# Pacing the dense pieces of an attention training step by TensorE time, fusing the q, k and v transposes, loading operand slabs by quarter, and moving VectorE work to ScalarE and GpSimd

## The chip, the cores and the metric

The kernel runs on one core of a Trainium2 chip. The metric is device microseconds of one execution. A ratio of two kernels is the mean time of the fast runs of one over the mean of the fast runs of the other, both from the same rounds on the same chip, so it is not quite the ratio of the medians that are quoted beside it. "About the same" means within 2%.

## The reference, cut to what matters

The program is forward and backward of four layers over 2048 tokens of width 640 with 32 heads of 20: linear attention (A), window attention (B), A, B. It returns the output and the gradients of the input and of the four weight matrices.

```python
def _A_ref(x, wqkv, wo):            # linear attention
    ...
    pq, pk = phi(q), phi(k)
    kv = jnp.einsum("bhsd,bhse->bhde", pk, v)
    ...
    return (num / den) ... @ wo

def _B_ref(x, wqkv, wo):            # causal window of 256
    scores = jnp.einsum("bhqd,bhkd->bhqk", q, k) * (Dh ** -0.5)
    mask = (idx[:, None] - idx[None, :] >= 0) & (idx[:, None] - idx[None, :] < W)
    p = _softmax(jnp.where(mask[None, None], scores, -1e9), axis=-1)
    return jnp.einsum("bhqk,bhkd->bhqd", p, v) ... @ wo

x = x + _A_ref(_layernorm(x), A_wqkv, A_wo)
x = x + _B_ref(_layernorm(x), B_wqkv, B_wo)     # and the same pair once more
```

## The kernel before

A tile is 128 tokens, so there are 16 tiles. Two kinds of stage matter here. A *forward pair* runs the output side of layer A, the whole layer B and the first side of the next layer A. A *window backward* runs the backward of layer B, in eight chunks of two tiles, with the output-side backward of B ahead of it and the rest of the backward behind it.

Both are written in the same way. A main sequence of short attention *steps* (8 per forward tile, 32 per chunk) needs ScalarE, VectorE and GpSimd between its matmuls. Between two steps the program emits *pieces* of dense work (projections, transposes, layer norms) from generators, so that TensorE has something to do while a step waits. Each `yield` ends a piece. The kernel before gives out pieces **by count**:

```python
def drive(main, fills):             # fills: (generator, pieces per step, delay)
    live = [[f[0], f[1], 0.0, f[2] if len(f) > 2 else 0] for f in fills]
    for _ in main:                  # one step of attention
        for f in live:
            f[3] -= 1
            if f[0] is None or f[3] >= 0:
                continue
            f[2] += f[1]
            while f[2] >= 1.0:
                f[2] -= 1.0
                if next(f[0], StopIteration) is StopIteration:
                    f[0] = None
                    break
    ...                             # what is left is emitted at the end

# forward pair, tile t: the front of a later tile and the back of the one before
    fills.append((take(ahead, 17), 17 / G))              # G = 8 steps
    fills.append((prev, 14 / (G - 2), 2))
    drive(self.b_core(st, lb, t, o), fills)

# window backward, chunk c
    fills.append((before(c + 1), 18 / 32))
    fills.append((behind(c - 2), 36 / 25, 7))            # two chunks late, from step 7
    drive(core(c), fills)
```

The pieces that make q, k and v of a forward tile, with a DMA transpose for q and k as soon as they are there, and one for v at the end:

```python
hn = self.ln(st, l, t, x)                                # VectorE, one piece
yield
hnT = self.flip(st.ps, st.sb, hn, "hnT", P, DT, P, nc.vector)
yield
for j, nm in enumerate("qkv"):
    for c in range(2):
        ps = self.dense(st, hnT, W, j * D + c * CW)      # 5 matmuls of 320 columns
        ...                                              # copy to R["s"] on VectorE
        yield
    if j == 1:
        self.dma(R["T"][:, 0:2, :, :]..., R["s"][:, 0:2, :, :]..., transpose=True)
self.dma(sv["s"][t], R["s"]...)
self.dma(R["T"][:, 2, :, :], R["s"][:, 2, :, :]..., transpose=True)
self.dma(sv["T"][t], R["T"]...)
```

In the window backward, half of the transposes of `ds` are done on TensorE and copied out of PSUM by VectorE; the others go by DMA. The trailing pieces `behind(c)` begin with a transposing DMA that reads what an earlier DMA stored (`dqT<-dqkv`), and their matmuls read `dqT`.

```python
nc.vector.tensor_copy(v(dT), v(ps))                      # dsT, VectorE
...
nc.vector.tensor_tensor(out=pr[:, hs, :], in0=self.heads(ps[:, 0:CW]),   # product for delta
                        in1=self.heads(o[:, c * CW:(c + 1) * CW]), op=ALU.mult)
...
with self.tc.high_priority():                            # score matmuls, exponential and ds
    ...                                                  # are placed ahead of the pieces
```

The order of instructions on an engine is fixed when the program is built, by a scheduler that takes the order of emission and these priorities.

The softmax here doesn't subtract the row's maximum and nothing guards it: scores larger than these inputs give would overflow.

## Time and profile before

| | us |
|---|---|
| time, median of 3 runs | 2978.84 (2966.33 to 2979.95) |
| profiled run | 2969.4 |
| forward: both pairs, from about 124 us to the first exponential of the first window backward | 843 |
| windows: both window backwards, each from its first exponential to its close | 1296 |
| the rest: first layer, two linear backwards, weight gradients | 830 |

These stage lengths are read from the trace by the start times of the instructions named; the forward stages begin at the first write of `mz`, at about 124 us.

First, three lines of the page of the kernel before: TensorE's busy time with its share of the span, and the granted TensorE clock and the DMA share by fortieths of the span, in tenths.

```profile
PE 2296.9 (77%) x28216; PEld 1520.9 (51%) x28216; DVE 1649.3 (56%) x3436; ACT 1104.7 (37%) x1693; POOL 775.9 (26%) x1584
...
PEclk9988888778886557777776985677877769989799
...
DMA  6264554456566567777655985676776457379852
```

TensorE is the busiest engine, and its clock is lower where the window backwards are. The next view gives busy time by stretch for the kernel before: first pair, second pair, first window backward. The columns are length, then busy us and number of instructions of PE, PEld, DVE, ACT and POOL, then the mean granted clock, the DMA share and GB/s.

```profile
124.00:585.00 461.00, 370.79 (x4800) 247.36 (x4798) 275.73 (x735) 214.05 (x227) 170.26 (x282) 0.85 0.50 143
585.00:944.00 359.00, 277.47 (x4131) 183.33 (x4130) 177.78 (x467) 176.26 (x129) 159.82 (x263) 0.81 0.59 162
944.00:1623.00 679.00, 499.32 (x7248) 333.66 (x7248) 450.66 (x744) 274.72 (x480) 214.99 (x500) 0.70 0.67 148
```

In the forward pairs TensorE is far ahead of the others; in the windows VectorE comes close to it (450.66 against 499.32 us). What TensorE waits for is told by the waits of the kernel before: total us, number, longest. First in the steady part of the second pair (660 to 900 us), then in four steady chunks of the first window backward (1172 to 1474 us).

```profile
PE ops L162 <- DVE ob L411: 8.2, 11, 0.8
PE flip L208 <- DVE o L318: 8.2, 12, 0.7
PE flip L208 <- DVE hn L229: 7.4, 12, 0.6
PE sT L162 <- DMA T<-s: 6.8, 12, 1.0
```

```profile
PE dp L162 <- DVE ds L655: 19.5, 35, 1.6
PE acc L162 <- DMA dsT<-ds: 13.2, 12, 2.4
PE dense L162 <- DMA dqT<-dqkv: 6.5, 4, 1.9
...
PE flip L661 <- DVE ds L655: 4.4, 8, 0.6
```

The forward waits are short and spread. In the windows the wait for `ds` on VectorE is the largest (by two readers, the product `dp` and the TensorE transposes `flip`: 23.9 us together), and that for the transposed `dsT` second.

### The profile page before, as it was taken

The page shows a single profiled execution, that of the slowest core. Times are in us where ns is not written, and L with a number is a line of the kernel's source. Part 1 is how long each engine was busy: PE and PEld are TensorE (multiplying, and loading weights), DVE is VectorE, ACT ScalarE, POOL GpSimd, SP SyncE. Part 2 cuts the span into 40 slices and gives each one's busy share as a digit, 9 for nine tenths or more (in the row PEclk, how much of TensorE's full clock was granted, in tenths as well). Part 3 has the DMA queues.
Part 4 walks back from the last instruction along what each step waited for, and adds up shares of the span by engine and source line. Part 5 has one row for each costly group of instructions (what it writes and reads, how often), then busy time and mean ns, then how long its engine had stood idle before and what let it go on. Part 6 is the DMA issues. An engine that isn't in the chain of part 4 may idle for free.

```text
span 2969.4 us, 68304 instructions
## 1 busy us (share of the span) xinstructions
PE 2296.9 (77%) x28216; PEld 1520.9 (51%) x28216; DVE 1649.3 (56%) x3436; ACT 1104.7 (37%) x1693; POOL 775.9 (26%) x1584
## 2 busy tenths in 40 slices
PE   5778888668885677877776856778777759968599
PEld 4455555445553455555554644555555536447454
DVE  6656666545552467777764654777777630037100
ACT  2245555325553344444441423444444300024000
POOL 2033443325553243333330003433433200000000
PEclk9988888778886557777776985677877769989799
DMA  6264554456566567777655985676776457379852
GB/s 231 95 175 140 145 158 146 133 160 164 160 167 159 163 136 147 163 150 163 136 128 152 272 218 159 141 155 166 165 162 129 102 167 228 117 207 262 270 161 73
DMA packets 737911, 484.46 MB, mean 163 GB/s; under 512 B 484160, under 2 KB 710464, under 8 KB 737600
## 3 DMA queue, kind: packets, MB, share of 16 engines
q1 hardware_dynamic: 737600, 480.10, 62.6%
q8 instruction: 222, 3.64, 0.5%
q14 instruction: 89, 0.73, 0.1%
HBM read 216.53 MB, written 146.54 MB: 122 GB/s over the span
## 4 chain that ended last, share of the span: by engine, by line
PE 29%; DMA 14%; DVE 8%; issue 8%; POOL 4%; ACT 2%; SPq 2%; POOLq 0%; ACTq 0%; DVEq 0%
PE wg L162 12%; PE dense L162 9%; DMA dsT<-ds 4%; DVE ds L655 4%; DMA dqT<-dqa 3%; DMA dqT<-dqkv 3%; PE dp L162 2%; POOL e L618 2%; PE acc L162 2%; SPq L134 2%; DMA dqkv<-dq 2%; POOL e L622 2%; PE flip L661 1%; PE flip L208 1%; ACT e L615 1%
## 5 line engine op out<-in xcount | busy, mean ns | idle before, releaser
L655 DVE TENSOR_TENSOR ds<-dp,e 128x768 bf16<-128x768 f32 (+2 forms) x512 | 462.3, 903 | 212.9 <-PE s L162 112.5
L615 ACT ACTIVATE e<-s 128x768 bf16<-128x768 f32 (+2 forms) x512 | 395.0, 771 | 496.0 <-PE s L162 362.3
L376 ACT ACTIVATE eT<-sT 128x1536 bf16<-128x1536 f32 (+2 forms) x256 | 351.0, 1371 | 343.5 <-PE sT L162 328.9
L618 POOL TENSOR_SCALAR_AFFINE_SELECT e<-e 128x256 bf16<-128x256 bf16 x512 | 214.7, 420 | 702.4 <-ACT e L615 681.6
L378 POOL TENSOR_SCALAR_AFFINE_SELECT eT<-eT 128x512 bf16<-128x512 bf16 x256 | 164.3, 642 | 417.2 <-ACT eT L376 417.0
L162 PE MATMUL acc<-qs,ds 128*128 128x20 bf16 x2880 | 259.6, 177 | 15.3 <-DVE dq L717 12.7
L162 PE MATMUL dp<-vT,dT 32*128 32x384 bf16 (+2 forms) x1024 | 208.6, 400 | 80.0 <-DVE ds L655 62.7
L162 PEld LDWEIGHTS <-dqT 128*128 128x128 bf16 x1920 | 183.4, 105 | 162.4 <-DMA dqT<-dqkv 42.2
L162 PE MATMUL acc<-ks,dsT 128*128 128x20 bf16 x2880 | 207.1, 177 | 71.2 <-DMA dsT<-ds 70.2
L162 PEld LDWEIGHTS <-hnT 128*128 128x128 bf16 x1920 | 194.3, 107 | 129.9 <-DVE hnT L213 27.1
L162 PE MATMUL wg<-rq,lh 128*128 128x480 bf16 x1280 | 259.5, 366 | 0.0
L162 PE MATMUL acc<-ds,e 128*128 128x20 bf16 x2880 | 255.0, 175 | 0.0
L939 DVE CAST wr<-wg 128x480 bf16<-128x480 f32 (+1 forms) x36 | 21.7, 602 | 369.8 <-PE wg L162 369.8
L162 PEld LDWEIGHTS <-ds 128*128 128x128 bf16 x2880 | 213.0, 101 | 20.3 <-issue 15.9
L162 PE MATMUL dense<-WTB,dqT 128*128 128x320 bf16 x960 | 185.0, 343 | 40.2 <-DMA dqT<-dqkv 39.6
L162 PEld LDWEIGHTS <-e 128*128 128x128 bf16 x2880 | 205.0, 101 | 18.4 <-issue 10.5
L162 PE MATMUL s<-kT,qT 32*128 32x384 bf16 (+2 forms) x1024 | 208.3, 404 | 1.5 <-ACT e L615 1.1
L661 PE MATMUL flip<-ident,ds 128*128 128x128 bf16 x1440 | 177.9, 265 | 38.6 <-DVE ds L655 35.4
L162 PEld LDWEIGHTS <-dsT 128*128 128x128 bf16 x2880 | 154.6, 102 | 101.4 <-DMA dsT<-ds 81.1
L162 PEld LDWEIGHTS <-lh 128*128 128x128 bf16 x1280 | 125.2, 98 | 133.7
L162 PE MATMUL dense<-WTA,dqT 128*128 128x320 bf16 x960 | 166.9, 311 | 33.3 <-DMA dqT<-dqa 33.3
L622 POOL TENSOR_SCALAR_AFFINE_SELECT e<-e 128x256 bf16<-128x256 bf16 x448 | 192.0, 429 | 0.0
(133 smaller groups left out, 4099.9 us busy)
## 6 DMA issues: line engine op xcount, KB each, us to landing
rq<-dqkv SPq DMA_DIRECT2D x16, 1920.0 KB, 9.5
s<-s SPq DMA_DIRECT2D x32, 768.0 KB, 4.3
T<-T SPq DMA_DIRECT2D x32, 768.0 KB, 3.6
dqkv<-dq SPq DMA_DIRECT2D x32, 480.0 KB, 3.8
dqkv<-dqa SPq DMA_DIRECT2D x32, 480.0 KB, 3.7
kT<-T SPq DMA_DIRECT2D x28, 512.0 KB, 3.7
vT<-T SPq DMA_DIRECT2D x28, 512.0 KB, 4.3
ks<-s SPq DMA_DIRECT2D x28, 512.0 KB, 4.4
```

The costliest lines, as they stand in the source:

```text
L134: return self.nc.sync.dma_start(out=out, in_=in_, transpose=transpose)
L162: return self.nc.tensor.matmul(out, lhsT=lhsT, rhs=rhs, start=start, stop=stop, skip_group_check=True, **kw)
L208: self.nc.tensor.transpose(t[0:w, j, :], src[:, c0:c0 + w], self.ident)
L376: nc.scalar.activation(e[:, :, 0:nb * P], s[:, :, 0:nb * P], ACT.Exp)
L378: nc.gpsimd.affine_select(out=dg, in_=dg, compare_op=ALU.is_ge, fill=0.0, base=0, pattern=[[0, 4], [1, P]], channel_multiplier=-1)
L615: ex = nc.scalar.activation(e[:, :, 0:cw], s[:, :, 0:cw], ACT.Exp)
L618: nc.gpsimd.affine_select(out=dg, in_=dg, compare_op=ALU.is_ge, fill=0.0, base=0, pattern=[[0, 2], [-1, P]], channel_multiplier=1)
L622: nc.gpsimd.affine_select(out=fr, in_=fr, compare_op=ALU.is_ge, fill=0.0, base=-1, pattern=[[0, 2], [1, P]], channel_multiplier=-1)
L655: st.frees.append(nc.vector.tensor_tensor(out=ds[:, :, 0:cw], in0=st.dp[:, :, 0:cw], in1=e[:, :, 0:cw], op=ALU.mult))
L661: nc.tensor.transpose(ps[:, 3 * j + i, :], ds[:, j, i * P:(i + 1) * P], self.ident)
L939: nc.vector.tensor_copy(r[:, 0:w], a[:, 0:w])
```

## The change

Its intent: give out pieces by the TensorE time they take, so that every step gets about the same; load the operands of the windows in fewer, longer DMAs; take work off VectorE in the windows. The core of the diff, with cuts:

```diff
-def drive(main, fills): ...
+class Pace:
+    def __init__(self, gen, rate): ...
+    def step(self):
+        self.acc = min(self.acc + self.rate, 2 * self.rate)
+        while self.acc > 0:
+            w = next(self.gen, StopIteration)
+            ...
+            if w is None:           # not yet: ends the step
+                return
+            self.acc -= w           # w: TensorE us of the piece
 ...
         hn = self.ln(st, l, t, x)
-        yield
+        yield 0.05
         hnT = self.flip(st.ps, st.sb, hn, "hnT", P, DT, P, nc.vector)
-        yield
+        yield 0.3
 ...                                 # dense pieces: yield 0.7; delta and its product: yield 0.02
-            if j == 1:
-                self.dma(R["T"][:, 0:2, :, :]..., transpose=True)
-        self.dma(R["T"][:, 2, :, :]..., transpose=True)
+        self.dma(R["T"]..., flat, transpose=True)         # q, k and v in one, at the end
 ...
+            fa = Pace(chain(*[front(t) for t in range(1, TT)]), 7.6 / G)
+            fb = Pace(behind(), 7.3 / G)
 ...
-                for nm, k, w in (("kT", "T", 1), ("vT", "T", 2), ("ks", "s", 1)): ...
-                for nm, k in (("qT", "T"), ("qs", "s")): ...
+                for nm in ("T", "s"):                     # q, k, v of 4 tiles, a quarter of the heads
+                    S[nm] = sl.tile([P, 4, 2, 3, P], BF, name="slab" + nm)
 ...
-            nc.vector.tensor_copy(v(dT), v(ps))
+            if (g + bi) % 2:
+                nc.scalar.copy(v(dT), v(ps))
+            else:
+                nc.vector.tensor_copy(v(dT), v(ps))
 ...
-            nc.vector.tensor_tensor(out=pr[:, hs, :], ...)   # per half, from PSUM
+        nc.gpsimd.tensor_tensor(out=pr, in0=dn[:, :, 0:DH], in1=self.heads(o), op=ALU.mult)
 ...
-                    fills.append((before(c + 1), 18 / 32))
-                    fills.append((behind(c - 2), 36 / 25, 7))
+            fb = Pace(all_behind(), 14.5 / 32)            # behind(c) from the moment c is stored
+                    paces.append(Pace(before(c + 1), 5.4 / 32))
```

The tiles of `dqT` and two other loads of the trailing pieces also get a second buffer. The fillers of the linear backwards are paced as well. I call the two moves off VectorE "the relief" below.

## The prediction

> What bounds the kernel now. Cutting the trace into stretches: first layer 0-124 us, two forward pairs 124-950 (826 us), two window-attention backwards (950-1624 and 1740-2427, 1361 us), two linear backwards about 236 us, weight gradients the rest. The change touches the forward pairs and the window backwards.
>
> Forward pair: TensorE is busy 371 of 462 us at a granted clock of 0.85; ScalarE (214) and VectorE (276) are below it. Window backward, steady part: 84 us per pair of tiles (32 steps), VectorE busy 63-67, TensorE 67 at clock 0.78, ScalarE 40. Its TensorE waits in 1118-1540: 28 us for ds on VectorE, 7 us for flip after ds, 20 us for the transposed dsT, 9 us for dqT. So TensorE is first, VectorE a close second. The clock records hold only 1.0 and 0.5; stretches with little matmul work in them are followed by 0.5. The Trainium skill's "TensorE: Matmul & The Clock Gate" (Part 1) says the same.
>
> What the change does.
> 1. Pacing. Read from the built instruction order: before, each forward tile has seven score groups with about 1.3 us (warm) of TensorE work between them, then one lump of 6.6 us. After, the lump is still there: 5.4-8.9 us in most tiles of the first pair, 2.2 in one; the tail after the last score group grows from 21 to 27 us. Work is unchanged. In the window backward the largest gap between score groups grows from 3.0 to 4.8 us. Worth: 0 to +10 us.
> 2. One transpose for q, k and v. Scores now wait for it after the last v piece; before they waited for q,k after the k pieces. TensorE has 3.0-4.0 us of work in between against 3.9 before, and the transpose is half as large again (T landed in a median 4.7 us). The wait "sT for T", 25 us over both pairs now, should roughly double: +15 to +30 us.
> 3. Slabs: per pair of tiles 6.3 MB instead of 4.2, in 1536 B rows rather than 1024 B. The 1024 B packets took 53 ns each and 14% of the DMA engines; I estimate 21%, DMA share 0.68 to 0.75. Waits for dsT: 0 to +10 us per window.
> 4. VectorE relief: per 84 us, eight dsT copies (0.55 us) to ScalarE and four products (0.48 us) to GpSimd: 6.3 us less, 10% of its work; its lumps between ds products shrink (4.3 to 3.6 us). ScalarE gets about 6 us more, with room. I expect a third to a half of the 35 us ds waits per window to go: -15 us each. Double-buffered dqT takes most of its 9 us: -8 us each.
> 5. The drain (about 73 us per window) gets the GpSimd product (1.35 us for 0.48) into a serial chain: +3 us each.
>
> Sum: forward +15 to +35, windows -50 to -10: near nothing.
>
> Predicted 2965 us, range 2885 to 3045. Faster by over 2%: 0.27; within 2%: 0.56; slower by over 2%: 0.17.
>
> What would show it: window stretches at 80-83 us per pair of tiles with VectorE near 58-60 busy; "dp for ds" waits clearly below 28 us; forward pairs unchanged or longer, with longer waits of sT on T; DMA share up 0.05-0.08 in the window.
>
> What would make it wrong: fewer VectorE stalls lifting the window clock well above 0.78 (faster); the fused transpose costing less because the score groups run further ahead (faster); low-work runs of steps dropping the clock, or slab bursts delaying dsT (slower).

## The result, and the profile after

The changed kernel took 3095.28 us in the median of three runs (3090.24 to 3097.12); the ratio to before is 1.040, with a 95% interval of 1.0354 to 1.0447. It is slower, and outside the predicted range. The forward stages went from 843 to 928 us and the windows from 1296 to 1341; the rest did not change (830 to 827).

The same three kinds of view for the changed kernel. Its page, then the stretches (first pair, second pair, first window backward):

```profile
PE 2310.6 (75%) x28216; PEld 1528.2 (49%) x28216; DVE 1573.1 (51%) x3244; ACT 1186.5 (38%) x1821; POOL 813.7 (26%) x1616
```

```profile
124.00:629.00 505.00, 376.90 (x4802) 248.38 (x4800) 284.46 (x737) 213.68 (x227) 170.36 (x282) 0.83 0.45 131
629.00:1030.00 401.00, 294.56 (x4130) 189.09 (x4130) 180.76 (x466) 176.15 (x129) 158.96 (x263) 0.75 0.50 145
1030.00:1728.00 698.00, 493.34 (x7248) 333.13 (x7248) 410.36 (x649) 315.25 (x544) 234.23 (x516) 0.71 0.71 166
```

VectorE lost 40 us of work in the window, as it should, and the stretch still grew by 19 us. In the second pair the number of matmuls is the same to one, the stretch grew by 42 us, and the clock fell from 0.81 to 0.75. TensorE idles more, so I look at its waits in the changed kernel, in the second pair (690 to 1000 us) and in the four chunks of the first window backward (1258 to 1572 us).

```profile
PE sT L163 <- DMA T<-s: 26.1, 11, 2.9
PE ops L163 <- POOL eT L381: 13.3, 18, 1.5
PE flip L209 <- DVE hn L230: 7.6, 11, 1.2
```

```profile
PE dp L163 <- DVE ds L654: 24.7, 42, 1.4
PE dense L163 <- DMA dqT<-dqkv: 17.5, 4, 4.7
PE acc L163 <- DMA dsT<-ds: 12.9, 8, 2.8
PE dp L163 <- DVE ds L532: 7.7, 4, 1.9
```

Per 100 us of the stretch, the wait of the scores (`sT`) for their transposed operands (`T`) went from 2.8 to 8.4 us. In the windows the wait of `dp` for `ds` grew, but `flip` no longer waits for it, so that the two together (24.7 us; 23.9 before) did not shrink although VectorE has less to do. The wait for `dqT` nearly tripled.

One tile boundary of the second pair shows the first point. The columns are start, duration, engine and instruction; SPq is the DMA queue, so its line is the issue of the transpose. Before, only the transpose of q and k stands in front of the scores of the next tile:

```profile
793.53 1.88 SPq L134 DMA_TRANSPOSE T<-s  x1
...
797.85 0.29 PE L162 MATMUL sT<-T,T 32*128 32x128 bf16 x8 [0.41 <-DMA T<-s]
```

After, at the same tile, the single transpose of q, k and v takes longer, already to issue (over all tiles the median issue is 4.0 us instead of 1.9):

```profile
857.50 4.08 SPq L135 DMA_TRANSPOSE T<-s  x1
...
865.14 0.40 PE L163 MATMUL sT<-T,T 32*128 32x128 bf16 x8 [2.74 <-DMA T<-s]
...
865.77 1.45 ACT L375 ACTIVATE eT<-sT 128x1536 bf16<-128x1536 f32 x1 [6.01 <-PE sT L163]
```

From issue to scores it is 4.3 us before and 7.6 us after, and TensorE waits 0.41 and then 2.74 us of that. ScalarE stood idle for 6.01 us (1.23 us before).

The second point is a stretch of the changed kernel's window backward: one exponential starts at 1285.24 us and the next only at 1297.75. The next three chunks have such a gap (11.8 to 12.1 us) at the same step:

```profile
1282.00 6.46 SPq L135 DMA_TRANSPOSE dqT<-dqkv  x1
...
1285.24 0.81 ACT L614 ACTIVATE e<-s 128x768 bf16<-128x768 f32 x1 [0.62 <-PE acc L163]
...
1286.29 0.50 PE L163 MATMUL s<-slabT 32*128 32x384 bf16 x2
...
1291.39 1.52 PE L163 MATMUL dense<-WTB,dqT 128*128 128x320 bf16 x5 [4.60 <-DMA dqT<-dqkv]
...
1293.34 2.07 PE L163 MATMUL dense<-WTB,dqT 128*128 128x320 bf16 x7
1293.59 0.80 ACT L664 COPY dsT<-flip 128x768 bf16<-128x768 bf16 x1 [7.54 <-PE flip L660]
...
1297.75 0.80 ACT L614 ACTIVATE e<-s 128x768 bf16<-128x768 f32 x1
```

TensorE stands for 4.60 us in front of a dense piece whose `dqT` is still in flight. The Trainium skill says in "TensorE: Matmul & The Clock Gate" (Part 2, Step-by-step) that "The MATMULs themselves stay in program order", and that only weight loads are pulled ahead. The trace agrees: nothing overtakes the waiting piece. When `dqT` lands, 15 of its matmuls, five of another piece and six transposes of `ds` follow in one lump, before the next accumulating matmuls of the attention (`acc`). By then ScalarE has been idle for 7.54 us.

### The profile page after: what moved, and what is told of

The parts are those of the page before. It is cut to its first block, busy times and chain, and to the rows that moved or that the text cites. A ratio compares the mean times of both kernels' runs of the same rounds, so it can differ in the third digit from the quotient of the medians.

```text
span 3095.4 us, 68187 instructions
## 1 busy us (share of the span) xinstructions
PE 2310.6 (75%) x28216; PEld 1528.2 (49%) x28216; DVE 1573.1 (51%) x3244; ACT 1186.5 (38%) x1821; POOL 813.7 (26%) x1616
## 5 line engine op out<-in xcount | busy, mean ns | idle before, releaser
L163 PE MATMUL dp<-slabT,dT 32*128 32x384 bf16 (+2 forms) x1024 | 205.3, 392 | 124.6 <-DVE ds L654 81.5
L163 PE MATMUL acc<-slabs,dsT 128*128 128x20 bf16 x2880 | 211.5, 176 | 73.1 <-DMA dsT<-ds 72.3
L163 PE MATMUL acc<-slabs,ds 128*128 128x20 bf16 x2880 | 256.0, 176 | 7.8 <-ACT dq L726 3.1
L163 PE MATMUL dense<-WTB,dqT 128*128 128x320 bf16 x960 | 201.4, 352 | 68.6 <-DMA dqT<-dqkv 67.7
L163 PEld LDWEIGHTS <-e 128*128 128x128 bf16 x2880 | 200.3, 100 | 19.6 <-issue 7.0
L163 PE MATMUL s<-slabT 32*128 32x384 bf16 (+2 forms) x1024 | 204.3, 396 | 3.4 <-DMA slabT<-T 2.4
L163 PE MATMUL dense<-WB,hnT 128*128 128x320 bf16 x960 | 190.1, 347 | 7.8 <-DVE hnT L214 5.8
```

The source lines that it names most:

```text
L163: return self.nc.tensor.matmul(out, lhsT=lhsT, rhs=rhs, start=start, stop=stop, skip_group_check=True, **kw)
```

## The experiments

Eighteen kernels were run. All gave correct results. The table has all of them, with the stage lengths of their profiled run and, where they were timed, the median and the ratio.

| run | forward | windows | median us | ratio to before, 95% interval |
|---|---|---|---|---|
| before | 843 | 1296 | 2978.84 | |
| the change | 928 | 1341 | 3095.28 | 1.040, 1.035 to 1.045 |
| pace_only | 892 | 1306 | 3034.02 | 1.024, 1.020 to 1.029 |
| half_transposes | 865 | 1318 | 3001.96 | 1.013, 1.008 to 1.018 |
| fused_and_relief | 906 | 1240 | 2977.12 | 1.004, 1.000 to 1.008 |
| pace_half | 888 | 1356 | 3076.03 | 1.038, 1.034 to 1.042 |
| relief_only | 845 | 1251 | 2919.64 | 0.983, 0.981 to 0.985 |
| relief_all_copies | 846 | 1259 | 2925.19 | 0.988, 0.984 to 0.991 |
| act_copies_paced_low | 940 | 1270 | 3042.35 | one run |
| pool_product_low | 914 | 1274 | 3019.47 | one run |
| front_paced_relief_paced | 891 | 1297 | 3015.89 | one run |
| lead_and_late_behind | 902 | 1282 | 3010.04 | one run |
| v_first_before_paced | 851 | 1292 | 2973.43 | one run |
| spaced_paced_relief | 841 | 1343 | 3015.91 | one run |
| spaced_after | 864 | 1393 | 3082.02 | 1.034, 1.030 to 1.038 |
| behind_paced | 844 | 1315 | 2993.86 | one run |
| cap_or_spacing | 916 | 1196 | 2940.72 | one run |
| busiest_engine_paced | 843 | 1312 | 2983.30 | one run |
| spaced_forward_counted_windows | 838 | 1244 | 2909.76 | 0.978, 0.973 to 0.983 |
| step_ends_both | 841 | 1196 | 2870.65 | 0.969, 0.966 to 0.971 |

The forward stages and the windows are separate in time, so a kernel often tests one thing in the first and another in the second.

### First round: which part of the change costs what

The two candidate causes were the pacing and the new layout (fused transpose forward, slabs in the windows).

**pace_only** has the new pacing, with transposes, loads and VectorE work as before (single buffers too, because the second ones did not fit beside the old loads).

```diff
-drive(self.b_core(st, lb, t, o), fills)
+drive(self.b_core(st, lb, t, outs[t]), [fa, fb])      # Pace, both stages
```

> The new pacing alone in all stages; layout, both transposes, the slab loads and the VectorE work as before (and single-buffered dqT, hn and g, for space). In the changed kernel the forward part (from 124 us to the first exponential of the window backward) grew by 85 us, and each window backward by 20 to 24 us. Theory F1 (one transpose for q, k and v costs the forward time): forward within 15 us of before. Rival F2 (the order in which paced pieces come costs it): forward +60 to +85 us. Backward, theory B1 (larger slab bursts on the DMA queue): windows within 6 us of before. Rival B2 (pacing leaves a larger TensorE lump): windows +15 to +25 us each.

Forward 892 (+48 us), windows 1306 (+10, within the spread). Pacing alone makes the kernel slower. The forward result lies between what the two theories said; the windows lie in the range of B1.

**half_transposes** has the new slabs and no pacing or relief, and transposes q, k and v in two halves by heads.

```diff
-for j, nm in enumerate("qkv"):
-    for c in range(2): ...
+for c in range(2):
+    for j, nm in enumerate("qkv"): ...
+    self.dma(R["T"][:, 4 * c:4 * c + 4]..., flat[:, c * 12 * P:(c + 1) * 12 * P], transpose=True)
```

> Old pacing, new layout, new slab loads, VectorE work as before; in the forward part q, k and v are made half by half, and each half of the heads is transposed as soon as its three pieces are out, in two transposes. F1: the scores of the first heads wait for a transpose half as long, issued two or three pieces earlier, so forward is 0 to 25 us shorter than before. F2: forward as before within 10 us, since the pacing is the old one. Backward: B1 says windows +15 to +25 us each, B2 says within 6 us of before.

Forward 865 (+22), outside both ranges; windows 1318 (+22, so 11 each, between the ranges of B1 and B2). The slabs cost on their own: in about 320 us of the window their packets of 1536 B took 85.1 us of the 16 engines at a mean of 80.6 ns, where the packets of 1024 B had taken 47.6 us at 53.2 ns.

**fused_and_relief** is the kernel before with the fused transpose in the old layout and the relief.

```diff
-            if j == 1:
-                self.dma(R["T"][:, 0:2, :, :]..., transpose=True)
-        self.dma(R["T"][:, 2, :, :]..., transpose=True)
+        self.dma(R["T"]..., R["s"]..., transpose=True)
```

> Old pacing, old layout, old slab loads. Forward: only the two transposes replaced by one behind v. F1: forward +60 to +85 us, the gap between the exponentials at a tile's end 11 us in the first pair and 5.8 us in the second as in the changed kernel (before: 8.4 and 2.8). F2: within 10 us of before. Backward: only the VectorE relief (half of the dsT copies on ScalarE, the product on GpSimd). If the relief helps as predicted, windows are 10 to 20 us shorter each; rival B3 (ScalarE copies delay the exponential): longer by 10 us or more.

Forward 906 (+62), windows 1240 (-56). The fused transpose alone costs more than the prediction gave it, as F1 said, and the relief alone gives more than the 10 to 20 us a window expected here. With the pacing the two forward costs are not additive: 48 and 62 alone, 85 together.

**pace_half** has pacing, slabs and half transposes without the relief.

```diff
-nc.scalar.copy(v(dT), v(ps))            # and the product back on VectorE
+nc.vector.tensor_copy(v(dT), v(ps))
```

> The changed kernel with the half-by-half transposes in the forward part, and the VectorE relief undone in the backward. F1: forward at least 60 us shorter than the changed kernel, so close to before. F2: forward within 20 us of the changed kernel. Backward has new pacing and new slabs: if both B1 and B2 hold, windows are longer than in either alone; against the changed kernel the difference is the relief alone, 0 to 15 us longer.

Forward 888, 40 us below the changed kernel, which neither theory said; windows 1356 (+60), and 15 us above the changed kernel, as expected. Alone, slabs and pacing cost 22 and 10 in the windows; together (with the second buffers) they cost 60.

### Second round: the relief, and first theories about the pacing

**relief_only** is the kernel before with nothing but the two moves off VectorE.

```diff
-nc.vector.tensor_copy(v(dT), v(ps))
+if (g + bi) % 2: nc.scalar.copy(v(dT), v(ps))
+else: nc.vector.tensor_copy(v(dT), v(ps))
```

> The kernel before with the VectorE relief alone. In the first runs, stage by stage: forward 843 us before, 892 with pacing alone, 905 with one transpose alone, 928 with both (the changed kernel); the two windows 1296 us before, 1306 with pacing alone, 1318 with slabs alone, 1356 with pacing and slabs, 1341 with all three, 1240 with relief alone. If stages add up, this kernel has forward 843 and windows 1240, so about 55 us (1.8%) less than before in all. Rival: the forward change of that run somehow helped the windows; then less than 30 us.

Windows 1251 (-45), ratio 0.983: within 2% of before, but clear of the noise, and well ahead of the changed kernel. In four chunks TensorE's waits are:

```profile
PE dp L162 <- DVE ds L654: 15.9, 28, 1.5
PE flip L660 <- DVE ds L654: 9.3, 12, 1.1
...
PE acc L162 <- DMA dsT<-ds: 3.8, 6, 0.8
```

The wait of `dp` for `ds` fell from 19.5 to 15.9 us, but that of `flip` rose from 4.4 to 9.3, so the waits for `ds` did not shrink (23.9 and 25.2 us together). What fell is the wait for `dsT`, from 13.2 to 3.8 us. The gain is therefore not where the prediction put it.

**act_copies_paced_low** and **pool_product_low** have each half of the relief alone in the windows, and take the priority of the score matmuls away forward, with pacing in the first and without it in the second.

```diff
-            with self.tc.high_priority():
-                for i in range(nb): ...         # scores, forward
+            for i in range(nb): ...
 # windows of act_copies_paced_low
+            if (g + bi) % 2: nc.scalar.copy(v(dT), v(ps))
 # windows of pool_product_low
+        nc.gpsimd.tensor_tensor(out=pr, in0=dn[:, :, 0:DH], in1=self.heads(o), op=ALU.mult)
```

> Backward: of the relief only the dsT copies on ScalarE, old pacing and loads: if the copies are the larger part, windows are 35 to 50 us shorter together; if the product is, under 20 us. Forward: pacing with both transposes as before, but the score matmuls lose their high priority, so that they stand where pacing puts them (the largest TensorE run between score groups in most middle tiles falls from 6-8 us to 2.5-5 us). Theory F3 (priority pulls score groups together and defeats pacing): forward at most 870 us, against 892 with priority. Rival: without priority ScalarE starves, forward over 900 us.

> Backward: of the relief only the product on GpSimd: windows 5 to 20 us shorter together if it is the smaller part. Forward: the kernel before with no priority for the scores: control for the run beside it. The largest TensorE run stays at 5.5 us. If priority itself costs time, forward is under 835 us; if it only matters with pacing, 843 to 870 us.

Each half gives about half: 1270 (-26) and 1274 (-22), which neither expectation had. Without priority the forward stages get longer, 940 against 892 with pacing and 914 against 843 without. So taking the priority away does not win back what pacing costs; theory F3 is out.

**front_paced_relief_paced** paces the front of a tile and counts its back forward; in the windows it has pacing and relief with the old loads.

```diff
-drive(self.b_core(st, lb, t, outs[t]), [fa, fb])
+drive(self.b_core(st, lb, t, o), [fa, Fill(prev, 14 / (G - 2), 2)])   # Fill: by count
```

> Forward: only the pieces ahead of a tile are paced, those behind it drip as before: if the later, shorter lead of the front is what pacing costs, forward is near 892 us as with both paced; if the paced pieces behind cost it, near 843 us. Backward: relief and pacing without slabs (and without double buffers): if the losses simply add up, windows 1240 + 10 = 1250 us; if pacing takes the gain of the relief away by itself, 1280 us or more, and if pacing only hurts together with slabs, 1255 or less.

Forward 891, as with everything paced (892): it is the front. Windows 1297, where relief alone has 1251: beside the relief, pacing costs 46 us, not 10.

### Third round: lead, lateness, order

**lead_and_late_behind** gives the fronts of two tiles during tile 0, to let the later ones run further ahead, and starts the dense part of the trailing pieces later.

```diff
-drive(..., [fa, fb])
+drive(..., [fa, fa, fb] if t == 0 else [fa, fb])
-                yield 0.4                       # behind: after the loads
+                yield 1.2
-            fb = Pace(all_behind(), 14.5 / 32)
+            fb = Pace(all_behind(), 17 / 32)
```

> Forward: both sides paced, both transposes as before, but two tiles' front pieces are given out in tile 0 as the kernel before does (with pacing alone the front had about one tile of lead). If the shorter lead is what pacing costs (F4), forward falls from 892 us to 843-860. If it is the piece by piece timing (F5), it stays at 880-900. Backward: relief and pacing, old loads, but the pieces behind a pair of tiles start later after its dq is stored (waits of 1.2 instead of 0.4 us, rate 17/32 instead of 14.5/32). Relief and pacing gave 1297 us for the two windows, relief with the old pacing 1251. If pacing costs because the pieces behind are put where dqT has not landed, so that they bunch up (B4), the windows fall to 1250-1270 us. If not, they stay at 1285-1305.

Forward 902, not shorter. The trace says that this was no test of a lead: the transpose of q and k was still issued only 5.3 and 5.0 us (means of the two pairs) before the first exponential of its tile, as in pace_only (5.4 and 5.2). Windows 1282: the later start, with a slightly higher rate, gives back 15 of the 46 us. That is between the two ranges expected, and little more than the spread.

**v_first_before_paced** makes v first and transposes it early, so that only the short transpose of q and k comes last, without pacing; in the windows it paces only the pieces ahead, with relief.

```diff
-for j, nm in enumerate("qkv"):
+for j, nm in ((2, "v"), (0, "q"), (1, "k")):
```

> Forward: old pacing, old layout, two transposes, but v is made first and q, k last, so the transpose that the scores wait for is issued behind all six pieces, as the fused one is, and is only as long as before. The fused one alone cost 62 us (843 to 905). If lateness is its price, forward is 880-905 us here; if its length is, 840-860. Backward: relief, old loads, only the pieces ahead (bd of the next pair) paced, those behind drip as before. B4: windows 1245-1265 us, since the pieces behind are the old ones. Rival (pacing of the pieces ahead costs it): 1280-1300 us.

Forward 851 (+8). So it is the length of the last transpose that the fused version pays for, more than its coming last. Windows 1292: pacing the pieces ahead alone takes 41 of the 45 us of the relief away.

**relief_all_copies** moves every `dsT` copy to ScalarE.

```diff
-if (g + bi) % 2: nc.scalar.copy(v(dT), v(ps))
-else: nc.vector.tensor_copy(v(dT), v(ps))
+nc.scalar.copy(v(dT), v(ps))
```

> The kernel before with relief taken further: all dsT copies of flips on ScalarE, not half. Relief alone gave 0.983 of the time before, windows 1251 us. Half of the copies was worth 26 us in windows. ScalarE is then near 195 of 300 us busy: if VectorE is still the tighter one, windows fall to 1225-1245 us and the ratio to 0.975-0.981; if the exponential now waits behind copies, windows 1250-1290 us.

Windows 1259, no better than half of them (1251) within the spread.

### Fourth round: the distance between producer and reader

By now pacing was known to cost 48 us forward and 46 us beside the relief, and not why. A new theory: counted pieces are also *spacers*. Before, a layer norm, a transpose with its copy, or a delta took a whole place in the count (about two pieces a step from the front of a tile, 0.56 and 1.4 a step from the two window queues), so the piece that reads it came half a step or more later. Paced at 0.02 to 0.3 us, the reader follows in the same step, and TensorE, in order, waits for it.

**spaced_paced_relief** ends the step after each such producer, in both stages, and lets a queue save up four steps of its rate instead of two, so that it does not fall behind. Otherwise it is pacing with relief and the old transposes and loads.

```diff
-        self.acc = min(self.acc + self.rate, 2 * self.rate)
+        self.acc = min(self.acc + self.rate, 4 * self.rate)
         hn = self.ln(st, l, t, x)
         yield 0.05
+        yield None                              # ends the step
         hnT = self.flip(...)
         yield 0.3
+        yield None
```

> Pacing by TensorE time with the relief, loads and transposes as before, and a forced end of the step after each layer norm, transpose, delta product and delta, so that its reader comes one step later at the earliest. Spacing theory: forward stages at most 870 us (892 without the spacing, 843 before), the wait of the transposes for the normalised tile in the first pair at most 15 us (24.8 in pace_only, 11.2 before), window stages at most 1275 us (1297 without spacing, 1251 with relief alone). Rival, that the even pacing itself costs (steps with too little TensorE work, the rest bunched at the end of a tile): forward stages 885 to 900, window stages 1285 to 1305, with the wait for the normalised tile gone or not.

Forward 841: all of the 48 us came back. But the wait on the normalised tile did not shrink as the theory had it (29.6 us in the first pair; at most 15 was expected), and the windows went the wrong way, to 1343. What did change forward is when the transposes are issued: 7.4 and 13.8 us before the first exponential of the tile instead of 5.4 and 5.2 (means of tiles 3 to 14, counted from 0, in the two pairs; single tiles have either 5 to 8 or 11 to 19). But the kernel before has 5.0 and 5.0 us and takes 843 us, so a shorter lead is not what pacing had cost.

**spaced_after** is the changed kernel with the same edit.

> The changed kernel whole, with the same forced step ends. Spacing theory: forward stages at most 905 us (928 for the changed kernel), window stages at most 1320 us (1341), time at most 3060 us, a ratio to before of at most 1.03. Rival: forward stages 920 to 935, window stages 1330 to 1350, time 3080 to 3110 us, ratio 1.035 to 1.045.

Forward 864 (from 928), windows 1393 (from 1341); 3082.02 us, ratio 1.034. The forward half was as expected; the windows half missed again, above even the rival's range.

**behind_paced** paces only the trailing pieces in the windows, with relief.

```diff
-fills.append((behind(c - 2), 36 / 25, 7))
+fb = Pace(all_behind(), 14.5 / 32)
```

> Forward as before; window stages with the relief, the pieces ahead by count as before, the trailing pieces paced by TensorE time. If either half of the pacing alone loses the relief: window stages 1285 to 1300 us (1292 when only the pieces ahead were paced, 1251 with none paced). If it is the pieces ahead alone: at most 1262 us. Forward stages 838 to 852 us under both.

Windows 1315, outside the range on the slow side. Either half of the pacing alone loses the relief, and the two losses do not add up (64 and 41 alone, 46 together). This edit also starts the trailing pieces of a chunk when it is stored, and no longer at step 7; the two were not separated here, but step_ends_both below keeps the early start.

### Fifth round: taking the two edits apart

**cap_or_spacing** has the larger saving without step ends forward, and step ends with the old saving of two steps in the windows.

```diff
 # forward                                     # windows
-yield None        (cap 4 stays)               -cap = 4      (yield None stays)
+                                              +cap = 2
```

> Pacing with relief; forward without step ends but with four steps of saved rate, windows with step ends but only two. Forward: if the step ends brought it down from 892 to 841 us, it stays at 880 to 905 us; if the larger saving did, at most 860 us. Windows: in this build the largest lump of dense TensorE work between two score groups is about 2.5 us instead of 4.8. If lumps are what the pacing costs in the windows, at most 1270 us (1251 with relief by count, 1297 paced); if the saving of four steps caused the 1343 us alone, about 1290 to 1300 us; if step ends themselves cost there, over 1310 us.

Forward 916: a little above the expected range, and far from 841, so the step ends brought it down. Windows 1196: the step ends help there too, by 101 us against 1297, and the saving of four steps had caused the 1343.

**busiest_engine_paced** weights each piece by the engine that it keeps longest, with the late start of the trailing pieces and no step ends.

```diff
-        yield 0.02                              # layer norm backward, delta, product
+        yield 1.85                              # and 1.1, 1.0, 1.3; rates 28.1/32 and 10.6/32
```

> Forward as before; windows with relief, trailing pieces starting later, and each piece weighted by the engine it keeps longest (layer norm backward 1.1 and 1.85 us, delta 1.0, GpSimd product 1.3) instead of by TensorE. If the pacing costs because VectorE pieces of almost no TensorE time are released together: window stages at most 1265 us and TensorE's wait for ds in four steady chunks at most 20 us (22.5 in lead_and_late_behind, 15.9 in relief_only). If not: 1275 us or more.

Windows 1312, and the wait for `ds` 34.9 us in four chunks: not it.

**spaced_forward_counted_windows** joins the spaced forward stages with the counted windows and the relief.

> Forward paced with step ends after producers, transposes and loads as before, windows scheduled by count with the relief: their TensorE order is that of relief_only. If the two gains are independent: forward stages 835 to 850 us, window stages 1240 to 1262 us, time 2900 to 2930 us, a ratio to before of 0.975 to 0.987, equal to or up to 0.5% better than relief_only (0.9827).

838 and 1244 us, 2909.76 us, ratio 0.978: as expected.

**step_ends_both** has step ends in both stages, saving four steps forward and two in the windows.

```diff
+    def __init__(self, gen, rate, cap=2): ...
+            fa = Pace(chain(*[front(t) for t in range(1, TT)]), 7.6 / G, 4)
+            fb = Pace(behind(), 7.3 / G, 4)     # window queues keep cap=2
```

> Pacing by TensorE time in both stages with the relief, transposes and loads of before, step ends after producers, four steps of saved rate forward and two in the windows. If the missing distance was the loss: forward stages 832 to 848 us, window stages 1185 to 1215 us, time 2845 to 2885 us, a ratio to before of 0.958 to 0.972. If cap_or_spacing's windows were a chance of that one run or hang on its forward stages: window stages 1240 us or more, ratio 0.975 or more.

841 and 1196 us, 2870.65 us, ratio 0.969 (0.966 to 0.971), all inside the expected ranges. It is the fastest version, and it is paced by TensorE time, so pacing as such is not what costs. Its waits, in the second pair (650 to 900 us) and in four chunks of the first window backward (1156 to 1425 us), and the stretch of those four chunks:

```profile
PE flip L209 <- DVE hn L230: 14.1, 13, 1.9
...
PE sT L163 <- DMA T<-s: 1.7, 2, 1.4
```

```profile
PE dp L163 <- DVE ds L672: 17.0, 38, 1.7
PE acc L163 <- DMA dsT<-ds: 7.9, 6, 2.3
...
PE dense L163 <- DMA dqT<-dqkv: 2.6, 1, 2.6
```

```profile
1155.71:1424.71 269.00, 224.33 (x3766) 155.94 (x3763) 208.93 (x324) 161.74 (x271) 124.89 (x272) 0.85 0.79 177
```

For the same four chunks, the kernel before and the changed kernel have:

```profile
1172.17:1473.52 301.35, 240.87 (x3797) 164.72 (x3795) 232.42 (x376) 142.13 (x240) 114.02 (x264) 0.77 0.74 156
```

```profile
1257.66:1571.63 313.97, 239.19 (x3792) 166.80 (x3792) 210.98 (x329) 163.32 (x272) 123.29 (x272) 0.78 0.78 179
```

The windows of front_paced_relief_paced are the same but for the step ends. Its four chunks have:

```profile
1210.28:1512.95 302.67, 234.19 (x3792) 165.38 (x3792) 210.98 (x329) 164.10 (x272) 124.89 (x272) 0.80 0.71 157
```

```profile
PE dp L185 <- DVE ds L675: 31.3, 45, 1.6
PE dense L185 <- DMA dqT<-dqkv: 8.9, 4, 3.2
PE acc L185 <- DMA dsT<-ds: 8.9, 7, 1.9
```

With step ends the wait of `dp` for `ds` fell from 31.3 to 17.0 us, that for `dqT` from 8.9 to 2.6; the clock was 0.85 instead of 0.80, and TensorE's busy time was 10 us less with 0.7% fewer matmuls in the stretch. Forward, the wait of the scores on `T` has all but gone. The wait on the normalised tile stayed. So the lever of the spacing theory is shown, and its first reason, that the reader waits less for its own producer, is not.

What the step ends do instead can be read from the built instruction order and the traces. Between two score groups there is other work for TensorE. I count the columns of its matmuls at 2.4 per ns, the full rate that the Trainium skill gives in "TensorE: Matmul & The Clock Gate" (Part 1); these are estimates. The first column has the largest such lump of a chunk (mean of chunks 3 to 5 of the first window, counted from 0; the recorded texts count a little differently and have 3.0, 4.8 and 2.5 where this count has 2.3, 4.4 and 2.4). The next two columns are measured: of the 32 distances between the starts of two exponentials in a chunk, the longest, and the mean of the other 31 (chunks 3 to 6 of both windows).

| run | largest lump, us | longest distance, us | other distances, us | windows, us |
|---|---|---|---|---|
| step_ends_both | 2.4 | 5.4 | 1.99 | 1196 |
| relief_only | 2.4 | 4.6 | 2.13 | 1251 |
| lead_and_late_behind | 2.6 | 4.6 | 2.26 | 1282 |
| v_first_before_paced | 3.5 | 6.4 | 2.22 | 1292 |
| front_paced_relief_paced | 4.4 | 9.5 | 2.13 | 1297 |
| busiest_engine_paced | 4.4 | 7.2 | 2.27 | 1312 |
| behind_paced | 5.7 | 10.6 | 2.16 | 1315 |
| spaced_paced_relief | 5.0 | 12.8 | 2.13 | 1343 |
| before | 2.3 | 4.6 | 2.27 | 1296 |
| pace_only | 5.0 | 9.9 | 2.13 | 1306 |
| the change | 4.4 | 11.7 | 2.14 | 1341 |

The first eight have the relief and the old loads, and their lumps and windows come in nearly the same order. The measured columns say where the time goes. Pacing alone and the relief alone shorten the ordinary step equally, from 2.27 to 2.13 us, and both together no further. Pacing also adds one long block to each chunk. Together this accounts for the relief's gain vanishing beside the pacing. The saving of four steps and the slabs with second buffers lengthen just this block, and step ends with a saving of two remove most of it (one of 9.0 and 9.7 us is left in chunk 3 of the two windows) and bring the ordinary step to 1.99 us. The block opens with the wait for `dqT`. In chunks 4 to 6 of the first window of step_ends_both the first reader of `dqT` comes 6.3, 9.3 and 9.8 us after its load is issued, when it has landed (6.2, 6.6 and 8.0 us). In spaced_paced_relief TensorE comes to that reader too early in each of chunks 3 to 6 and waits 3.4 to 3.8 us. That the later reader is what removes the block fits this, but no run tests it alone. And not every loss is the block: three of the runs have ordinary steps of 2.22 to 2.27 us.

Forward, the same measure shows that pacing's loss stands at the boundary of two tiles (means of tiles 2 to 14 of the first and the second pair):

| run | last exponential of a tile to first of the next, us | first to last of a tile, us | forward, us |
|---|---|---|---|
| before | 8.4, 2.9 | 18.2, 17.3 | 843 |
| pace_only | 10.1, 4.1 | 18.0, 17.6 | 892 |
| fused_and_relief | 9.8, 5.3 | 19.6, 16.7 | 906 |
| the change | 11.4, 5.9 | 17.8, 16.9 | 928 |
| step_ends_both | 6.5, 2.9 | 20.0, 16.5 | 841 |

## Why the prediction was wrong

The prediction was 2965 us, the result 3095.28. Point by point:

1. **Pacing, "Worth: 0 to +10 us".** This is the step that failed most. Measured alone it is +48 us forward and +10 in the windows, and +46 in the windows beside the relief. The prediction had compared the lumps in the built order, found that the forward one "is still there" and the largest window one grown from 3.0 to 4.8 us, and priced that at almost nothing, because "Work is unchanged". The work was the same and its place was not: each forward tile boundary grew by 1.7 and 1.2 us in the two pairs (15 boundaries in each, so about 44 of the 48 us, an estimate), and each window chunk got a block of about 10 us where the longest distance had been 4.6. In the changed kernel that block is 12.5 us (1285.24 to 1297.75) and opens with a wait of 4.60 us on `dqT`. The same weights and rates with step ends after producers cost nothing forward (841) and gain in the windows (1196).
2. **Fused transpose, "+15 to +30 us".** The mechanism was right (scores wait for `T`: 2.8 to 8.4 us per 100 us in the second pair), the size was not. Alone it is +62 us, 1.9 us for each of 32 tiles where the range means 0.5 to 0.9; on top of the pacing it is +36 (928 against 892), and with step ends +23 (864 against 841). It took the transpose to be half as large again, but issue to scores grew by 3.3 us, from 4.3 to 7.6, at the boundary shown.
3. **Slabs, share 0.68 to 0.75, "0 to +10 us per window".** The share rose from 0.67 to 0.71 over the first window backward. The cost alone was 11 us per window, at the edge of the range; beside pacing and relief the difference is 22 per window (1341 against 1297; the second buffers are in it as well), and it stands in the block (9.5 to 11.7 us a chunk). The wait it named did not show it: `dsT` was 13.2 us before and 12.9 after.
4. **Relief, "-15 us each", and double buffering, "-8 us each".** The relief alone gave -45 to -56 us over both windows, so it was if anything underestimated, but not by the path named: the waits for `ds` did not shrink (23.9 and 25.2 us in four chunks), the wait for `dsT` did (13.2 to 3.8). And the estimate was added to the others as if independent. The pacing took the gain away: 1297 with both. The `dqT` term had the wrong sign: that wait went from 6.5 to 17.5 us in four chunks. Pacing alone has 10.4: its trailing pieces start when a chunk is stored, and TensorE comes to the first reader 4.2 to 4.6 us after the load's issue instead of 5.7 to 6.3. In the changed kernel the load also lands later, 7.8 to 9.3 us after its issue instead of 5.9 to 7.6 with pacing alone. A second buffer would not be expected to help against that.
5. **Drain, "+3 us each".** From the last exponential to the close: 83.8 and 83.3 before, 85.4 and 86.8 after. The number fits, by luck as far as the runs show: the relief alone, with its GpSimd product, shortened the drain (81.1 and 82.6), and pacing alone, without it, lengthened it (89.0 and 88.1).

The sum was therefore wrong in both stages: +85 us forward where +15 to +35 was said, +45 in the windows where -50 to -10 was said. More than half of the 85 us is the pacing alone (48), and the fused transpose adds the rest. In the windows pacing cancelled the relief (1297, where before has 1296), and the slabs with the second buffers came on top (+44). The signs it gave ("forward pairs unchanged or longer, with longer waits of sT on T") were seen; "dp for ds clearly below 28 us" was not: 24.7 us in 314 us is 7.9 per 100 us, where the 28 us in 422 us were 6.6.

Open: why a step end moves the forward transposes earlier (5.4 to 7.4 us and 5.2 to 13.8 us of lead) and shortens the tile boundary is not shown. Where the saving of four steps and the slabs beside the pacing cost time is seen, in the block, but not why it grows by so much. Whether a saving of two would do forward was not run. The one run with slabs and step ends (spaced_after) used the saving of four, so nothing is known of slabs in the windows of step_ends_both.

## What to carry to other kernels

When filler work is given out between the steps of a loop whose steps wait for one another, its schedule also sets the distance between producers and their readers; on an engine that takes its matmuls in order, a filler in front of an unlanded DMA stops the loop behind it. If you replace counting by a cost, keep the distances explicitly (here: end the step after each producer) and keep the saved-up credit small (in these windows four steps of it cost 147 us against two), then look at the longest distance between two steps of the loop, not at the mean. And don't add the gains of parts that share a critical path: here the relief was worth 45 us or nothing, depending on the pacing beside it.

## What the Trainium skill lacked or had wrong

- "TensorE: Matmul & The Clock Gate" (Part 1) says that activity moves the clock between two values only; the clock records agree, with only 0.5 and 1.0. What the page doesn't give is how a mean of them answers to the order of a loop's filler work: for nearly the same matmuls, four chunks had 0.77 before and 0.85 with step ends (240.87 and 224.33 us busy).
- "DMA: Bandwidth & Descriptors" (Latency and other measured facts) gives transposes 261 GB/s, or about 350 to 400 GB/s in the contiguous case, from which a transpose of 768 KB instead of 512 KB would take about 0.7 to 1.0 us longer (an estimate). Issue to scores grew by 3.3 us here, and the issue on the queue alone took 4.08 us instead of 1.88. The page has no issue time for a transpose on this chip that covers it.
- The same page (Why small descriptors are slow) gives a fixed cost of about 3 cycles per packet beside one for each 32 bytes, from which a packet of 1536 B would take 1.46 times as long as one of 1024 B (an estimate). Here it took 1.52 times as long, 80.6 to 53.2 ns, so the longer rows gained nothing.
- "TensorE: Matmul & The Clock Gate" (Part 2, Step-by-step) has that matmuls stay in program order, but no number for what a wrong order costs a loop: here a matmul that waited 4.60 us for its operand stood in a stretch of 12.5 us between the starts of two exponentials.
